# Attention in front of two soft mixtures on one Trainium2 core: the division by the sums, the narrowing of 64-bit weights and the order of all queues are changed

## The chip, the cores and the metric

One core of one Trainium2 chip. The core has TensorE (matrix products, written to PSUM), VectorE (DVE in the profile), ScalarE (ACT), GpSimd (POOL), the queue SP that issues most transfers, and 16 DMA engines. The metric is the device time of one execution in microseconds; the kernel before has a median of 676.77 us in three runs (672.96 to 681.78).

## The reference

```python
# q, k, v: (8, 8, 576, 64) float32
scores = scale * np.matmul(q, k.transpose(0, 1, 3, 2))          # scale = 1/8
scores = np.where(block_i >= block_j, scores, -1e9)             # causal in blocks of 64
scores = scores - np.max(scores, axis=-1, keepdims=True)
attn = np.exp(scores)
attn = attn / (np.sum(attn, axis=-1, keepdims=True) + 1e-09)
out = np.matmul(attn, v)                                        # -> x: (4608, 512)
# soft mixture: logits = x @ phi; softmax over tokens d, over slots c
# slot_input = d.T @ x; 8 experts (relu(slot_input @ w1[e]) @ w2[e]); x = c @ slot_out
# second block: a = x @ w1; b = x @ w2; result = ((a * b) @ w3) @ w_out
```

The weights of the second block come as 64-bit floats.

## The kernel before

The 64 heads are 32 pairs of two heads; the two heads of a pair lie in the upper and lower 64 partitions. Four pairs make a batch (one of the 8 examples). For each pair n the attention does, by the names of the planner:

- `ld`, `ldv`: load q and k (`raw`, 576 KB) and v (320 KB) on SP; `cast` (ScalarE) makes the high part, `sub` (POOL) the low part, so that products run in a fast format with a correction
- `M0` to `M3` (TensorE): rough scores of the high parts, for the maxima; `R0` to `R3` (VectorE) reduce them; `l2` masks the maxima of blocks and reduces again; `mT`, `mc`, `mx` transpose them, copy them out of PSUM and write them as a row (by DMA) into the operand that subtracts them
- `Q0` to `Q3` (TensorE): the scores in three products and that correction; `E0` to `E3` (ScalarE): exponentials into PTa, PTb, PTc
- `P0` to `P4` (POOL): partial sums of the exponentials; `SU` (TensorE) sums over partitions; `sb` (VectorE) adds the result to `Sb`
- `V1`, `V0` (TensorE): products with v; `c1`, `c0` (ScalarE) copy them to `xT`

For each batch b but the last: `sumT` transposes `Sb`, `r` takes reciprocals, `rT` and `rc` transpose them back and copy, `rw` writes them to HBM and `rd` reads them spread over partitions; `sx0` to `sx3` (VectorE) scale the four tiles of `xT`; then `lg` (logits), `lgT`, `L4`, the softmax over slots (`cm` to `cTd`), the softmax over tokens (`LT` to `dnc`), `xn`, `xc` (x in its natural layout) and `S`, `SSu` (slot inputs).

Beside all this, 16 narrowing jobs `b1` to `b4`, `bm` turn 64-bit weights of 128 x 512 into float32 by shifts and masks on VectorE, each loaded by `bl` (512 KB). `win` loads expert weights (2,048 KB) into tiles that the attention no longer needs; the first is loaded at the start. The constants of the start are 374 KB.

PSUM has two double tiles `sc` for Q, one double tile `mx` for M (and `LT`), and two single tiles `pv` for all the rest.

The order on each engine is not found by a scheduler: class `Plan` lists all these operations with engine, duration, what they wait for and a due time (`n * PERIOD + OFF[name]`), and `order()` runs them through a list scheduler; among operations that can start within `LOOK` of the first, the one with the smallest due time (plus `WAIT` for lateness) comes next. `run()` issues in that order, and each engine executes its own queue in order.

After the attention: the last batch's softmaxes (`push_tail`), eight experts with their weights loaded window by window, products of the second block's weights, and a last stage of products of 512 columns (L1210).

The functions that the change touches, with the lines of the profile:

Of the kernel before, what the change touches and what calls it, by code (L numbers as in the profile page):

```python
# [51 lines left out]
OFF = dict(ld=-59.98, ldv=-11.1, cast=-11.65, sub=-2.81, M0=-23.01, M1=-25.68, M2=-15.87, M3=-20.31, l2=61.69,  # L52
           mT=-12.75, Q0=16.46, Q1=14.73, Q2=17.44, Q3=10.38, P0=-30.76, P3=19.54, V1=14.16, V0=59.16, SU=15.87,
           sumT=-32.63, sx=11.53, lg=-1.05, lgT=24.25, cm=55.23, cT=15.16, LT=46.32, dn=40.78, xn=21.48, xstep=5.41,
           S=-15.63, b=30.37)
PERIOD, SWITCH, WAIT = 11.25, 2.51, 22.29
LOOK = dict(PE=0.13, DVE=0.94, ACT=0.32, POOL=2.58, SP=3.66)
BG0, BGS = 10.14, 1.42
MX = ((.26, 1.22), (.21, 1.1), (.15, .83), (.23, .83))
QK = ((1.26, 1.03), (1.03, 1.03), (.59, .71), (.48, .6))  # L60
SLOTS = {"sc": 2, "mx": 1, "pv": 2}


class Plan:
# [3 lines left out]
    def __init__(self, nb):  # L68
# [3 lines left out]
        quarter = lambda x: [f"{x}{i}" for i in range(4)]  # L72
        for n in range(N):
            self.due = lambda t: n * PERIOD + off[t]
            op = lambda name, *a, **k: self.op((name, n), *a, **k)
            at = lambda *names: [(x, n) for x in names]
            op("ld", "SP", .45, old(n - RAW, "sub"), lat=5.5 if n else 2.6)
            op("ldv", "SP", .45, old(n - VB, "V1", "V0"), lat=6)
            op("cast", "ACT", 1.16 if n else .7, at("ld") + old(n - NS, *quarter("Q")))
            op("sub", "POOL", 2.65, at("cast"))  # L80
            for i, (d, r) in enumerate(MX):
                op(f"M{i}", "PE", d, at("cast"), "mx", mode="rows")
                op(f"R{i}", "DVE", r, at(f"M{i}") + old(n - 2, "l2"), free=f"M{i}", due=f"M{i}")
            op("l2", "DVE", .55, at(*quarter("R")) + old(n - 2, "mT"))
            op("mT", "PE", .11, at("l2"), "pv")
            op("mc", "ACT", .25, at("mT") + old(n - 2, "mx"), free="mT", due="mT")
            op("mx", "SP", 1.9, at("mc") + old(n - 2, *quarter("Q")), lat=2.2, due="mT")
# [12 lines left out]
            op("V1", "PE", 2.05, at("E0", "E1", "E2", "ldv"), "pv", mode="cols")  # L100
            op("c1", "ACT", .43, at("V1") + x, free="V1", due="V1")
            op("V0", "PE", .68, at("E0", "E3", "ldv"), "pv", mode="cols")
            op("c0", "ACT", .38, at("V0") + x, free="V0", due="V0")
            op("SU", "PE", .69, at(*(f"P{j}" for j in range(5))), "pv", mode="quarters")
            op("sb", "DVE", .49, at("SU") + (old(n - 1, "sb") if n % NP_B else old(b - 1, "sumT")), free="SU", due="SU")
        for b in range(nb - 1):
# [21 lines left out]
            op("cT", "PE", .28, at("cmul"), "pv")  # L128
            op("cTc", "ACT", .46, at("cT") + old(b - 1, "cTd"), free="cT", due="cT")
            op("cTd", "SP", 1.2, at("cTc"), lat=3, due="cT")  # L130
            op("LT", "PE", .57, at("L4"), "mx")
            op("LTm", "DVE", 1.2, at("LT"), due="LT")
            op("LTe", "ACT", 2.0, at("LTm") + old(b - 1, "dn", "SSu", "Ls"), free="LT", due="LT", late=.1)
            op("Ls", "DVE", .16, at("LTe"), due="LT", late=.2)
            op("dn", "PE", .35, at("LTe"), "pv", mode="few rows")
            op("dnc", "ACT", .29, at("dn") + old(b - 1, "S"), free="dn", due="dn")
            for c in range(5):
                op(f"xn{c}", "PE", .45 if c < 4 else .3, at(*quarter("sx")), "pv", due="xn", late=c * off["xstep"])
                op(f"xc{c}", "ACT", .59, at(f"xn{c}", "lg"), free=f"xn{c}", due="xn", late=c * off["xstep"])
            op("S", "PE", 1.06, at("dnc", *(f"xc{c}" for c in range(5))), "pv", mode="quarters")  # L140
            op("SSu", "DVE", .75, at("S", "LTe"), free="S", due="S")
        for j in range(16):
# [3 lines left out]
            op("bl", "SP", .45, old(j - 1, "b3", "bm"), lat=4, due="b", late=-.5 * PERIOD)  # L146
            op("b1", "DVE", .6, at("bl") + old(j - 1, "b4"), due="b")
            op("b2", "DVE", .85, at("b1"), due="b", late=.1)
            op("b3", "DVE", .85, at("b2"), due="b", late=.2)
            op("bm", "ACT", .67, at("bl") + old(j - 1, "b4"), due="b")  # L150
            op("b4", "DVE", .85, at("b3", "bm"), due="b", late=.3)
        self.due = lambda t: t * PERIOD
# [1173 lines left out]
```

## Time and profile before

| | |
|---|---|
| median of three runs | 676.77 us |
| the profiled execution | 680.79 us, its span 679.0 us |
| TensorE busy | 607.6 us (89%) |
| VectorE busy | 482.9 us (71%) |
| ScalarE busy | 329.1 us (48%) |
| POOL busy | 365.5 us (54%) |
| moved by DMA | 117.00 MB, mean 172 GB/s |

Busy times are unions, so overlapping products count once. The chain that ended last puts 29% of the span on TensorE. The attention takes about the first 405 us. Rows of a timeline give the start, the duration of the group, the engine, the line and the operation, and in brackets how long the engine sat idle before it and who released it.

### The profile page before, as it was taken

What the parts mean: (1) busy time and instruction counts of PE and PEld (TensorE: products, weight loads), DVE (VectorE), ACT (ScalarE), POOL (GpSimd) and SP (SyncE); (2) the same over time, 40 slices, a digit from 0 to 9 for tenths busy, and PEclk for the clock granted to TensorE, in tenths of its full rate; (3) what the DMA queues carried; (4) which work ended last, traced back from release to release, by engine and by line L of the source; (5) the groups of instructions that cost most, each with busy time, mean ns of one, the idle gap of its engine ahead of it and who ended that gap; (6) DMA issues with size and microseconds to landing.
All of it is one profiled execution on the core that took longest, in us unless ns stands there. A gap on an engine that the chain in (4) does not pass through costs nothing. (4 is left out here: it accounts for less than half of the span.)

```text
span 679.0 us, 13657 instructions
## 1 busy us (share of the span) xinstructions
PE 607.6 (89%) x5414; PEld 437.1 (64%) x5414; DVE 482.9 (71%) x692; ACT 329.1 (48%) x628; POOL 365.5 (54%) x280
## 2 busy tenths in 40 slices
PE   3699879989889889889979998769999998999997
PEld 1577666766666666667757765425664676888886
DVE  5688787898898898885675535799933798555550
ACT  2356436646456456446645563345423335445451
POOL 4499686787587587587666650144424322332220
PEclk9999879989889899889989998988999998999999
DMA  8434722643543453442611729999884404555742
GB/s 304 172 106 136 197 87 60 161 138 109 132 150 98 135 157 96 128 133 72 169 57 45 207 94 410 419 367 429 318 307 171 127 1 125 188 192 193 260 147 93
DMA packets 40674, 117.00 MB, mean 172 GB/s; under 512 B 6639, under 2 KB 17031, under 8 KB 38547
## 3 DMA queue, kind: packets, MB, share of 16 engines
q1 hardware_dynamic: 40431, 116.06, 50.3%
q8 instruction: 42, 0.69, 0.4%
q14 instruction: 21, 0.17, 0.1%
q10 hardware_dynamic: 180, 0.07, 0.0%
HBM read 105.80 MB, written 10.47 MB: 171 GB/s over the span
## 5 line engine op out<-in xcount | busy, mean ns | idle before, releaser
L324 DVE TENSOR_REDUCE bm<-mx 128x10 f32<-128x640 f32 (+2 forms) x128 | 126.1, 985 | 61.2 <-PE mx L320 60.0
L359 PE MATMUL sc<-set 64*128 64x320 f32 (+4 forms) x1152 | 121.3, 321 | 0.0
L359 PEld LDWEIGHTS sc<-set 64*128 64x128 f32 x1152 | 96.2, 200 | 10.6 <-issue 7.2
L309 POOL TENSOR_TENSOR set<-raw,set 128x1152 fp32r<-128x1152 f32 x32 | 92.7, 2897 | 11.5 <-ACT set L302 9.7
L1210 PE MATMUL ops<-H,Ph 128*128 128x512 f32 x288 | 91.6, 399 | 3.3 <-ACT H L1114 2.4
L320 PE MATMUL mx<-set 64*128 64x320 f32 (+4 forms) x384 | 59.1, 359 | 23.3 <-DVE bm L324 22.2
L378 POOL TENSOR_TENSOR acc<-PTa,PTb 128x640 f32<-128x640 f32 x32 | 53.6, 1674 | 44.6 <-ACT PTb L367 39.1
L1185 POOL TENSOR_TENSOR Pl<-rot,Ph 128x384 fp32r<-128x384 f32 x24 | 30.3, 1281 | 77.4 <-ACT Ph L1183 77.4
L1210 PEld LDWEIGHTS ops<-H,Ph 128*128 128x128 f32 x288 | 55.0, 191 | 17.3 <-ACT H L1114 2.9
L359 PE MATMUL sc<-shift 64*128 64x320 f32 (+4 forms) x384 | 61.1, 313 | 0.0
L378 POOL TENSOR_TENSOR acc<-acc,PTc 128x640 f32<-128x640 f32 x31 | 53.8, 1736 | 12.0 <-ACT PTc L367 10.1
L320 PEld LDWEIGHTS mx<-set 64*128 64x128 f32 x384 | 33.8, 198 | 38.0 <-DVE bm L324 24.5
L1210 PE MATMUL ops<-H,Pl 128*128 128x512 f32 x144 | 57.6, 400 | 0.0
L367 ACT ACTIVATE PTc<-sc 128x512 f32<-128x512 f32 x64 | 41.3, 645 | 33.1 <-PE sc L359 33.1
L906 PE MATMUL wps<-wo,w 128*128 128x512 f32 x192 | 51.3, 411 | 3.1 <-POOL wo L852 1.7
L458 DVE TENSOR_TENSOR xT<-xT,shift 128x576 f32<-128x576 f32 x28 | 48.7, 1796 | 3.4 <-DMA shift<-rr 3.4
L1213 ACT COPY o<-ops 128x512 f32<-128x512 f32 x36 | 21.1, 587 | 58.5 <-PE ops L1212 58.2
L906 PEld LDWEIGHTS wps<-wo,w 128*128 128x128 f32 x192 | 35.3, 192 | 20.7 <-issue 5.8
L367 ACT ACTIVATE PTb<-sc 128x1024 f32<-128x1024 f32 x32 | 32.8, 1024 | 27.2 <-PE sc L359 27.2
L393 PE MATMUL pv<-PTc,v 128*64 128x256 f32 (+1 forms) x256 | 44.9, 429 | 0.3 <-DVE Sb L421 0.3
L378 POOL TENSOR_TENSOR acc<-PTa,PTc 128x256 f32<-128x256 f32 x31 | 28.1, 906 | 27.5 <-ACT PTc L367 27.4
L367 ACT ACTIVATE PTa<-sc 128x1024 f32<-128x1024 f32 x32 | 32.8, 1026 | 16.4 <-PE sc L359 16.3
(247 smaller groups left out, 1217.3 us busy)
## 6 DMA issues: line engine op xcount, KB each, us to landing
win<-in_moe_w SPq DMA_DIRECT2D x16, 2048.0 KB
raw<-in_qk SPq DMA_DIRECT2D x32, 576.0 KB
v<-in_v SPq DMA_DIRECT2D x32, 320.0 KB
rot<-cs SPq DMA_DIRECT2D x48, 192.0 KB
out<-o SPq DMA_DIRECT2D x11, 768.0 KB
raw<-in_moe_w SPq DMA_DIRECT2D x16, 512.0 KB
w3raw<-in_w3T SPq DMA_DIRECT2D x16, 512.0 KB
shift<-rr SPq DMA_DIRECT2D x14, 576.0 KB
```

Source lines behind the costliest of these rows:

```text
L309: self.nc.gpsimd.tensor_tensor(lo, self.raw.pop(n), hi.bitcast(F32), op=ALU.subtract)
L320: self.nc.tensor.matmul(self.mx_b[:, h, o:o + kn], lhsT=qh[r, q0:q0 + 128], rhs=kh[r, k0:k0 + kn], start=True, stop=True)
L324: self.nc.vector.tensor_reduce(self.bmb[n % 2][:, :, o:o + m // 64], self.mx_b[:, :, 0:m].rearrange("p h (n k) -> p h n k", k=64), axis=AX ...
L359: self.nc.tensor.matmul(ps[:, h, o0:o0 + w], lhsT=lt[r, k] if i < 3 else lt[r], rhs=rt[r, q0:q0 + w], start=i == 0, stop=i == 3)
L367: self.nc.scalar.activation(out=out, in_=ps[:, :, 0:sum(g[3] for g in self.UNITS[u])], func=AF.Exp, scale=SCALE)
L378: eng.tensor_tensor(acc[:, :, lo:hi], a, b, op=ALU.add)
L393: mm(ps[64 * h:64 * h + 64, q0 - lo:q1 - lo], lhsT=v[:, 128 * j + 64 * h:128 * j + 64 * h + 64], rhs=pt[:, h, o:o + q1 - q0], start=j == 0 ...
L458: self.nc.vector.tensor_tensor(x, x, self.rb[:, p], op=ALU.mult)
L906: nc.tensor.matmul(p, lhsT=a[:, o], rhs=b, start=c + i == 0, stop=c == 7 and i == 2)
L1185: eng.tensor_tensor(Pl[:, k], p, Ph[:, k].bitcast(F32), op=ALU.subtract)
L1210: nc.tensor.matmul(ps, lhsT=a[:, k, r], rhs=b[:, k], start=n == 0, stop=False)
L1213: nc.scalar.copy(o[:, t], ps)
```

## The change

1. **Division.** `sumT`, `rT`, `rw`, `rd` go. `r` is one reciprocal of the whole `Sb` (128 x 320) into a `pv` tile; `rc` and `rl` combine it into the operand `rA`, `rb0` to `rb4` spread it over partitions by a product with a selection matrix `rsel`, into `pv` tiles, and `sx0` to `sx4` multiply `xT` by them from there. EPS is added in the batch's last `sb`.
2. **Narrowing.** The working tile `u` of `b1` to `b4` is a `pv` tile in place of one in SBUF.
3. **Masking.** The masked maxima are overwritten by two constant writes in place of an addition of `lmask`.
4. **PSUM.** `mx` is gone; three double tiles `sc` serve M, Q and LT.
5. **Start.** The constants are loaded by a planned operation `kl`, and `kc`, `kd`, `ke` build what is made of them.
6. **Plan.** Due times depend on the pair's place in its batch, TensorE takes its operations strictly by due time, `LOOK` and `WAIT` are new for each engine; waits for buffers have moved from the copies to the products in front of them.

```diff
-OFF = dict(ld=-59.98, ldv=-11.1, cast=-11.65, sub=-2.81, M0=-23.01, ...
+OFF = dict(ld=(-216.25, -345.22, 6.22, 92.03), ldv=(29.88, 253.15, 394.31, -307.64), cast=(46.44, 145.88, 221.53,
...
-SLOTS = {"sc": 2, "mx": 1, "pv": 2}
+SLOTS = {"sc": 3, "pv": 2}
...
+            if n == 0:
+                op("kl", "SP", 2.9, [("ld", 1)], lat=2.3, due="ld")
+                op("kc", "ACT", 2.2, at("cast", "kl"), due="cast", late=.1)
...
-                op(f"M{i}", "PE", d, at("cast"), "mx", mode="rows")
+                op(f"M{i}", "PE", d, at("cast") + old(n - 2, "l2"), "sc", mode="rows")
...
-            op("sumT", "PE", .33, [("sb", last)], "pv")
-            op("r", "DVE", .78, at("sumT") + old(b - 1, "rT"), free="sumT", due="sumT")
-            op("rT", "PE", .11, at("r"), "pv", due="sumT", late=.1)
...
-                op(f"sx{p}", "DVE", .8, at("rd") + [("c1", NP_B * b + p), ("c0", NP_B * b + p)], due="sx", late=.1 * p)
+            op("r", "DVE", 2.8, [("sb", last)] + old(b - 1, *(f"rb{i}" for i in range(5))), "pv")
+            op("rc", "ACT", .46, at("r"), due="r", late=.1)
+            op("rl", "DVE", .5, at("rc"), free="r", due="r", late=.2)
...
+                op(f"rb{i}", "PE", .3 if i < 4 else .43, at("rl") + x + [("kd", 0), ("ke", 0)], "pv")
+                op(f"sx{i}", "DVE", .65 if i < 4 else .4, at(f"rb{i}"), free=f"rb{i}", due=f"rb{i}")
...
-            op("b1", "DVE", .6, at("bl") + old(j - 1, "b4"), due="b")
+            op("b1", "DVE", .6, at("bm"), "pv", due="b")
...
     def op_l2(self, n, _):
-        t = self.st_p.tile([128, 2, 45], F32, tag="l2", name="l2")
-        self.nc.vector.tensor_tensor(t, self.bmb[n % 2], self.lmask, op=ALU.add)
+        t = self.bmb[n % 2]
+        for i in (8, 24):
+            self.nc.vector.memset(t[0:64, :, i:i + (6 if i == 8 else 12):5 if i == 8 else 11], -1e30)
...
+    def op_r(self, b, slot):
+        ps = self.st["r"] = self.pv_b[slot][:, 0:320]
+        self.nc.vector.reciprocal(ps, self.Sb[:, 0:320])
...
+    def op_rl(self, b, _):
+        self.nc.vector.scalar_tensor_tensor(self.rA, self.st["r"], self.low[:, 0:1], self.rT.bitcast(F32), op0=ALU.mult, op1=ALU.add)
+
+    def op_rb(self, b, slot, i):
+        ps = self.st["rb", i] = self.pv_b[slot]
+        for p, g, o, c, w in ((i, 0, 0, 0, 320), (i, 1, 320, 64, 192)) if i < 4 else [(p, 1, 64 * p, 256, 64) for p in range(4)]:
+            self.nc.tensor.matmul(ps[:, o:o + w], lhsT=self.rsel[:, g, p], rhs=self.rA[:, c:c + w], start=True, stop=True)
+
+    def op_sx(self, b, _, i):
+        ps = self.st["rb", i]
+        if i < 4:
+            x, r = self.xTb[b % 2][:, i, 0:512], ps
+        else:
+            x, r = self.xTb[b % 2][:, :, 512:S], ps[:, 0:256].rearrange("p (g t) -> p g t", g=4)
+        self.nc.vector.tensor_tensor(x, x, r, op=ALU.mult)
...
-            u = self.u64 = self.cv.tile([128, 512], I32, tag="u", name="u64")
+            u = self.u64 = self.attn.pv_b[slot].bitcast(I32)
```

What now stands where. VectorE, around the scaling of a batch in the middle, first in the kernel before (u is the narrowing's tile in SBUF, `shift` holds the factors read back from HBM):

```order
L324 TENSOR_REDUCE bm_119<-mx 128x2x7
L837 SCALAR_TENSOR_TENSOR wB<-m_2765,u_2735 128x512
L324 TENSOR_REDUCE bm_119<-mx 128x2x8
L458 TENSOR_TENSOR xT_130<-xT_130,shift 128x576 x4
L324 TENSOR_REDUCE bm_119<-mx 128x2x5
L421 TENSOR_TENSOR Sb<-Sb,pv_116 128x320
L828 TENSOR_SCALAR u_2971<-raw_2828 128x512
L830 SCALAR_TENSOR_TENSOR u_2971<-raw_2828,u_2971 128x512
L324 TENSOR_REDUCE bm_119<-mx 128x2x5
```

The same engine at the scaling in the changed kernel (pv_114 and pv_115 are the two small PSUM tiles, `shift` is rA):

```order
L852 SCALAR_TENSOR_TENSOR wB<-m_3178,pv_114 128x512
L453 SCALAR_TENSOR_TENSOR Sb<-pv_115,Sb 128x320
L460 RECIPROCAL pv_114<-Sb 128x320
L466 SCALAR_TENSOR_TENSOR shift<-pv_114,low,shift 128x320
L479 TENSOR_TENSOR xT_127<-xT_127,pv_114 128x512
L479 TENSOR_TENSOR xT_127<-xT_127,pv_115 128x512
L479 TENSOR_TENSOR xT_127<-xT_127,pv_114 128x4x64
L352 TENSOR_REDUCE bm_117<-sc_113 128x2x7
L479 TENSOR_TENSOR xT_127<-xT_127,pv_115 128x512
L479 TENSOR_TENSOR xT_127<-xT_127,pv_114 128x512
L352 TENSOR_REDUCE bm_117<-sc_111 128x2x5
L352 TENSOR_REDUCE bm_117<-sc_113 128x2x8
```

The narrowing's last step and the batch's addition now stand in front of one reciprocal, the scalings read PSUM, and one reduction stands between them.

TensorE, from Q0 of the next pair but one to the spread (L471) in the changed kernel; the sums of the batch's last pair (L437), a maxima transpose (L363) and Q2 (L388) stand directly ahead (sc are the three double tiles):

```order
L388 MATMUL sc_113<-set_65 128x448 x6
L388 MATMUL sc_113<-shift 128x448 x2
L388 MATMUL sc_113<-set_65 128x64 x6
L388 MATMUL sc_113<-shift 128x64 x2
L422 MATMUL pv_115<-PTc,v 64x320 x2
L422 MATMUL pv_115<-PTa,v 64x320 x2
L422 MATMUL pv_115<-PTb,v 64x320 x2
L422 MATMUL pv_115<-PTb,v 64x192 x2
L426 MATMUL pv_115<-PTa,v 64x64 x2
L388 MATMUL sc_112<-set_65 128x256 x6
L388 MATMUL sc_112<-shift 128x256 x2
L471 MATMUL pv_114<-shift 128x320
```

In the kernel before, the transposed sums stood there directly behind the slot inputs (L573), with the other transpose (L441) behind the next Q3, Q1 and Q2:

```order
L571 MATMUL pv_117<-xT_130,d 32x512 x4
L573 MATMUL pv_117<-xT_130,d 32x128 x4
L429 MATMUL pv_116<-ident,Sb 128x128 x3
L320 MATMUL mx<-set_68 128x320 x2
L359 MATMUL sc_114<-set_67 128x256 x6
L359 MATMUL sc_114<-shift 128x256 x2
L359 MATMUL sc_113<-set_67 128x320 x6
L359 MATMUL sc_113<-shift 128x320 x2
L359 MATMUL sc_113<-set_67 128x192 x6
L359 MATMUL sc_113<-shift 128x192 x2
L441 MATMUL pv_117<-ident,r 40x128
```

So four transposes have left TensorE's queue, and between the sums and the first product that needs the reciprocals stand a maxima transpose, the groups Q2 and Q0, a V1 and a Q3.

SP at the start, in the changed kernel (the constants are xT to sel):

```order
L316 DMA raw<-in_qk 128x1152 x2
L320 DMA v<-in_v 128x640 x2
L862 DMA win_160<-in_moe_w 128x4096
L320 DMA v<-in_v 128x640
L291 DMA xT_128<-in_rt_const 6x1216 x2
L292 DMA ident<-in_ident 128x128
L293 DMA phib<-in_phib 128x256
L294 DMA phi<-in_phi 128x128
L295 DMA sel_67<-in_sel 128x32
L316 DMA raw<-in_qk 128x1152 x2
L837 DMA raw_206<-in_moe_w 128x1024
```

and before:

```order
L289 DMA raw<-in_qk 128x1152
L266 DMA lmask<-in_lmask 128x90
L267 DMA ident<-in_ident 128x128
L265 DMA xT_130<-in_rt_const 6x1216 x2
L268 DMA phib<-in_phib 128x256
L269 DMA phi<-in_phi 128x128
L270 DMA sel_69<-in_sel 128x32
L289 DMA raw<-in_qk 128x1152
L293 DMA v<-in_v 128x640 x3
L822 DMA raw_174<-in_moe_w 128x1024
L847 DMA win_176<-in_moe_w 128x4096
L289 DMA raw<-in_qk 128x1152 x2
```

The constants stood behind the first `raw` and now stand behind two `raw`, three `v` and the first window.

## Rows read from the trace of the kernel before

**Rows 1.** Stretches: length, busy us of PE, PEld, DVE, ACT, POOL; PEclk, DMA share, GB/s.

```profile
257.40:309.00 51.60, 45.92 (x528) 34.38 (x524) 42.99 (x54) 28.11 (x53) 36.99 (x27) 0.93 0.40 118
...
356.80:405.10 48.30, 48.30 (x598) 35.97 (x593) 24.61 (x44) 29.60 (x61) 31.51 (x29) 1.00 0.35 102
sum 379.76, PE 348.20 PEld 259.09 DVE 294.46 ACT 212.41 POOL 276.40; mean PE 43.52 PEld 32.39 DVE 36.81 ACT 26.55 POOL 34.55
```

**Rows 2.** Waits of PE, 54.9 to 357 us: total us, times, longest.

```profile
PE pv L467 <- DVE xT L458: 15.4, 8, 2.3
PE mx L320 <- DVE bm L324: 8.3, 9, 3.0
PE pv L429 <- DVE Sb L421: 5.8, 3, 1.9
```

**Rows 3.** Timeline of DVE at the scaling of a batch.

```profile
292.57 7.07 DVE L458 TENSOR_TENSOR xT<-xT,shift 128x576 f32<-128x576 f32 x4
```

**Rows 4.** DVE lines over the span: durations ns min/median/max, first and last start.

```profile
L458 DVE TENSOR_TENSOR xT<-xT,shift x28: 746/1702/3184, 88.5 to 389.8; 128x576 f32<-128x576 f32 x28
L830 DVE SCALAR_TENSOR_TENSOR u<-raw,u x16: 681/1369/2997, 14.2 to 281.8; 128x512 int32<-128x512 int32 x16
L828 DVE TENSOR_SCALAR u<-raw x16: 419/818/1773, 13.1 to 280.7; 128x512 int32<-128x512 int32 x16
L421 DVE TENSOR_TENSOR Sb<-Sb,pv x24: 470/472/489, 49.4 to 407.5; 128x320 f32<-128x320 f32 x24
L437 DVE RECIPROCAL r<-r x7: 403/403/405, 68.9 to 372.0; 128x40 f32<-128x40 f32 x7
L499 DVE RECIPROCAL csm<-csm x7: 190/191/191, 106.2 to 404.3; 128x5 f32<-128x5 f32 x7
```

**Rows 5.** Timeline of PE: after a wait, and the same groups without one.

```profile
275.34 0.85 PE L359 MATMUL sc<-set 64*128 64x256 f32 x6
...
278.53 0.73 PE L359 MATMUL sc<-set 64*128 64x320 f32 x6
...
323.03 0.55 PE L429 MATMUL pv<-ident,Sb 128*128 128x128 f32 x3
...
323.76 0.51 PE L359 MATMUL sc<-set 64*128 64x256 f32 x6
...
325.56 0.71 PE L359 MATMUL sc<-set 64*128 64x320 f32 x6
```

**Rows 6.** Timeline of PE: Q0, M0, V1, M3, Q3, SU by their first rows.

```profile
280.56 0.88 PE L359 MATMUL sc<-set 64*128 64x448 f32 x6
...
281.85 0.50 PE L320 MATMUL mx<-set 64*128 64x192 f32 x4
282.28 0.76 PE L393 MATMUL pv<-PTc,v 128*64 128x320 f32 x4
...
284.48 0.42 PE L320 MATMUL mx<-set 64*128 64x256 f32 x4
284.74 0.60 PE L359 MATMUL sc<-set 64*128 64x256 f32 x6
...
285.39 0.30 PE L408 MATMUL pv<-PTc,ones 128*32 128x128 f32 x2
```

**Rows 7.** A stretch of the last stage, products of 512 columns.

```profile
590.00:640.00 50.00, 50.00 (x215) 40.30 (x215) 26.58 (x43) 23.41 (x49) 12.95 (x10) 1.00 0.62 210
```

**Rows 8.** Timelines of ACT and PE at the start: third cast, first maxima, first score product.

```profile
19.55 1.15 ACT L302 CAST set<-raw 128x1152 fp32r<-128x1152 f32 x1 [5.77 <-DMA raw<-in_qk]
20.61 0.25 ACT L339 CAST mT<-pv 10x128 fp32r<-10x128 f32 x1
...
25.34 1.35 PE L359 MATMUL sc<-set 64*128 64x448 f32 x6
```

**Rows 9.** A stretch of the expert stage.

```profile
460.00:480.00 20.00, 20.00 (x115) 13.57 (x112) 18.38 (x28) 8.85 (x16) 8.41 (x7) 0.93 0.99 407
```

**Rows 10.** The page's group of the exponentials of Q0.

```profile
L367 ACT ACTIVATE PTa<-sc 128x1024 f32<-128x1024 f32 x32 | 32.8, 1026 | 16.4 <-PE sc L359 16.3
```

More of the change, by code (lines that the diff above doesn't have):

```diff
@@ L99, in __init__ @@
             x = old(b - 2, "S", *(f"xn{c}" for c in range(5)))
[L100 to L105, printed above, removed]
+            op("V1", "PE", 2.05, at("E0", "E1", "E2", "ldv") + x, "pv", mode="cols")
+            op("c1", "ACT", .43, at("V1"), free="V1", due="V1")
+            op("V0", "PE", .68, at("E0", "E3", "ldv") + x, "pv", mode="cols")
+            op("c0", "ACT", .38, at("V0"), free="V0", due="V0")
+            op("SU", "PE", .69, at(*(f"P{j}" for j in range(5))) + ([] if n % NP_B else old(b - 1, "r")), "pv", mode="quarters")
+            op("sb", "DVE", .49, at("SU"), free="SU", due="SU")
         for b in range(nb - 1):
@@ L164, in order @@
         ops, INF = self.ops, 1e18
-        free = dict(PE=1., DVE=2., ACT=2., POOL=3., SP=.7)
+        free = dict(PE=4., DVE=2., ACT=2., POOL=3.5, SP=.7)
         slots, held, done, mode, out = {r: [0.] * n for r, n in SLOTS.items()}, {}, {}, None, []
         waits, then, ready = {k: len(o["after"]) for k, o in ops.items()}, {}, {e: {} for e in free}
+        row = deque(sorted((k for k in ops if ops[k]["eng"] == "PE"), key=lambda k: (ops[k]["due"], k)))
         for k, o in ops.items():
@@ L212, with __init__ @@
 class Attn:
-    def __init__(self, tc, ctx, io, nb, keep, after_scores=None, background=()):
-        self.after_scores, self.background = after_scores, background
+    def __init__(self, tc, ctx, io, nb, keep, rest, windows=True):
+        self.rest, self.windows = rest, windows
+        rest.attn = self
         self.tc, self.nc, self.io, self.nb = tc, tc.nc, io, nb
@@ L285, in constants2, with op_kl, op_kc, op_kd @@
             nc.gpsimd.memset(t[64:128, :, S:SP], 0.0)
+    def op_kl(self, n, _):
+        nc, io = self.nc, self.io
+        for h in range(2):
+            nc.sync.dma_start(out=self.stage[64 * h:64 * h + 6, 0:640 + S], in_=io["rt_const"])
+        nc.sync.dma_start(out=self.ident, in_=io["ident"])
+        nc.sync.dma_start(out=self.phib, in_=io["phib"])
+        nc.sync.dma_start(out=self.phi, in_=io["phi"])
+        nc.sync.dma_start(out=self.keep["sel32"], in_=io["sel32"])
+    def op_kc(self, n, _):
+        self.nc.scalar.copy(self.CT.rearrange("p a b -> p (a b)"), self.stage[:, 0:640])
+        for t in self.Xb:
+            self.nc.scalar.copy(t, self.xconst)
+    def op_kd(self, n, _):
+        v = self.ident.rearrange("p (g h x) -> p g h x", g=2, h=2)
+        for g in range(2):
+            a, b = (v[:, g, :, x:x + 4].unsqueeze(3).to_broadcast([128, 2, 4, 64]) for x in (0, 4))
+            self.nc.gpsimd.tensor_tensor(self.rsel[:, g].rearrange("p x (h d) -> p h x d", h=2), a, b, op=ALU.add)
+    def op_ke(self, n, _):
+        nc = self.nc
+        v = self.ident.rearrange("p (j x) -> p j x", x=32)
+        nc.vector.tensor_reduce(self.low[:, 0:1], v[:, :, 4:8], axis=AX.XY, op=ALU.add)
+        nc.vector.tensor_scalar(self.low[:, 1:2], self.low[:, 0:1], -2.0, 1.0, op0=ALU.mult, op1=ALU.add)
     def op_ld(self, n, _):
@@ L813, in narrow, with background @@
         return dst
-    def background(self, j, step):
+    def background(self, j, step, slot):
         nc = self.nc
@@ L1227, in setup @@
     keep["cs"] = dp.tile([48, nb * S], F32, name="cs")
-    keep["rr"] = [dp.tile([8, 640], F32, name=f"rr{i}") for i in range(2)]
     sp = ctx.enter_context(tc.tile_pool(name="sets", bufs=1, side="right"))
@@ L1248, in attn_only @@
         with ExitStack() as c2:
-            Attn(tc, c2, io, nb, keep, None, rest.background).run()
+            Attn(tc, c2, io, nb, keep, rest, False).run()
         rest.cv_ctx.close()
@@ L1259, in full @@
         with ExitStack() as c2:
-            Attn(tc, c2, io, nb, keep, rest.load_expert, rest.background).run()
+            Attn(tc, c2, io, nb, keep, rest).run()
         rest.run(out)
```

198 lines of the change are left out of this document (80 added, 118 removed).

## The prediction

> **What bounds the kernel now.** I read the page first: TensorE is busy 89% of the span and leads the chain, and a second stage behind the attention lives on transfers. The change lies in the attention, which ends at about 405 us, so I cut that part into its eight batches of four pairs [rows 1]. From the first score product at 25.34 us to 405.10 TensorE works 348.20 of 379.76 us, so it stands idle 31.6 us. The last batch has no idle time at all (48.30 of 48.30), one with narrowing on VectorE has 5.7 (51.60 less 45.92). So TensorE is the bound wherever it is fed, and what there is to gain is its waits. The view of waits [rows 2] says who causes them between 54.9 and 357 us: products of logits wait for the scaling of xT (15.4 us), maxima for the reduction that frees their only PSUM tile (8.3 us), and the transposed sums for VectorE's addition (5.8 us). These 29.5 us are nearly all of the 31.6, and VectorE ends every one.
>
> Why is VectorE late when it is busy only 71%? The timeline shows four scalings back to back that take 7.07 us [rows 3]; meanwhile no reduction runs and no maxima tile comes free. The same instruction took 0.75 us at best, 1.70 in the median and 3.18 at worst, and a step of the narrowing 0.68, 1.37 and 3.00. The addition into Sb, which has one input in PSUM and one in SBUF, took 0.470 to 0.489 us in all 24 cases [rows 4]. So instructions with two SBUF inputs are stretched by something that leaves those with a PSUM input alone; POOL works through the same stretch on SBUF tiles.
>
> A wait costs more than itself. After the last of the three waits for the sums (1.9 us) three score groups took from 275.34 to 278.53, 3.19 us; the same groups took 1.80 us (323.76 to 325.56) where nothing had waited: 1.39 us lost [rows 5]. [...]
>
> **The change part by part, in TensorE's time.**
>
> *Scaling and reciprocals.* The four scalings from SBUF (28 in all, 48 us by the median) become 28 of 512 columns and seven of 256 with the factor in PSUM. From the addition of 320 columns at 0.47 I scale to 0.7 and 0.4: 22 us. Against that VectorE now takes reciprocals of 320 columns. The reciprocal of 40 columns took 0.403 and that of 5 took 0.191, 6.06 ns a column, so 2.1 us; the other bound is 320/40 of 0.403, 3.2 us. With the combination after it (320 columns, 0.47) VectorE comes out some 8 us lower in total at 2.1 and about level at 3.2, but what counts is that no block of 7 us stands in its queue. The 15.4 us and the 5.8 us go; the write to HBM and the read back go too, and SP loses three issues a batch. TensorE pays: eight products of 320 or 192 columns and four of 64 in place of four transposes. A product of 512 columns takes 50.00/215 = 0.23 us in the last stage [rows 7]; two of half that width I take at 0.3, and the four small ones at 0.4, 1.6 together; the transposes that go took 0.55 for three [rows 5], so about 0.75 for four: +0.8 a batch, **+5.6 us** in seven (bounds 3 and 9).
>
> *Narrowing in PSUM.* Three of its four steps lose their second SBUF input and should take the 0.68 of their best case: 16 x (4 x 0.7) = 45 us against 16 x (0.82 + 3 x 1.37) = 79 by the medians, the last two steps taken like the second. No TensorE work depends on it, so its own gain is nothing; what it frees is the queue in front of reductions and sums. It now holds one of the two small PSUM tiles for about 2.8 us, twice a batch.
>
> [...] The first step, one input and a constant, had a best case of 0.419 in SBUF [rows 4], less than the 0.68 of the others. [...]
>
> *One pool of PSUM tiles.* Maxima may now take any of three double tiles. The 8.3 us of waits go with them. The price could be a score product that waits for a tile held by a reduction; in the new order a tile is asked for again only three groups later, and with no 7 us block ahead a reduction is done by then. I take none; the bound is the old 8.3.
>
> *Masking* by two constant writes in place of a sum, and the new constants built once: VectorE and POOL have room (42.99 and 36.99 of 51.60 in the fullest kind of batch), so nothing; above, 32 times the 0.47 of a whole addition, 15 us of VectorE, still off the path.
>
> *The clock.* The eleven waits of the first and third row of [rows 2] fall in nine places of over 1.3 us; at 1.2 us each, 11 us come back.
>
> *The start.* SP now issues the 2 MB window ahead of the constants. In the old order the third raw pair, behind 5.0 MB, had landed at 19.55 [rows 8]. The new constants end after 4.49 MB, where 5.62 were then through: 19.55 x 0.80 = 15.6 us. They are copied in three pieces (say 2 us), and the first maxima are written by DMA, which took from 20.61 to 25.34 at most, 4.7 us. So the first score product comes at about 22.5 instead of 25.34: **-2.5 us** (bounds -4 and +2).
>
> *New waits.* The tightest new chain is sums, addition, reciprocal, copy, combination, spread: 0.47 + 2.1 + 0.47 + 0.47 and five hand-overs that I put at 0.1, 4.0 us (5.1 with the dear reciprocal). In TensorE's new order Q2, Q0, V1 and Q3 stand between. Their start-to-start times are 1.29 for Q0, 2.20 for V1, 0.65 for Q3 [rows 6], and Q2, wider than Q3, at least that: 4.8 us. It fits, with 0.8 to spare or 0.3 too little. Other chains (maxima, DMA write, scores) have a whole pair's work between. No plan is kept to the tenth of a microsecond, so I charge 1 us a batch: **+7** (bounds 0 and 29, next part).
>
> Sum against the profiled execution (span 679.0, 680.8 with what lies around it): -15.4 - 5.8 - 8.3 - 11 = -40.5; +5.6 - 2.5 + 7 = +10.1; together -30.4, so 650.4. That execution lies 4.0 above the median of 676.77; against the median: 646.4, forecast **647 us**. The stage behind moves up with it: its transfers run at 407 GB/s with a share of 0.99 at 460 to 480 us [rows 9], but they start when the last scores release the windows, and that moment moves.
>
> **The rivals.**
>
> 1. *The new chain takes the place of the old wait.* ScalarE's copy of the reciprocals stands in its queue behind the exponential of Q0, 1.03 us [rows 10], which starts only when Q0 is done. If that and the dear reciprocal meet, the spread starts about 1.4 late, and with the clock's 1.2 it costs 2.6 a batch, 18 us; if the small tiles add as much again per narrowing, 29. Against -37.4 without new waits that leaves -19 to -8: 658 to 669. For it: the chain fits by tenths. Against: the order puts five microseconds of other products there.
>
> 2. *Slower: the narrowing stays stretched and now holds a PSUM tile.* If what stretches it isn't the second SBUF input but the strided int32 read (both stand in the same rows), the four steps keep 0.82 + 3 x 1.37 = 4.9 us, 2.1 over plan, and for that time TensorE has one small tile for V, SU, transposes and spread. With the clock that is up to 3.3 us, 16 times 53: 676.8 - 37.4 + 53 = 692. It decides (slower than before) from 2.3 us a narrowing. Against: the best case 0.68 has the same strides; the scalings have none and are stretched the same.
>
> 3. *Hidden.* The attention ends early but the later stage doesn't move. It would take loads that are already late by themselves; 0.99 in [rows 9] speaks for it, their release by the last scores against. 670 to 677.
>
> 4. *All waits go.* The same without the +7 and with the start's best bound: 638.
>
> **How the numbers follow.** Forecast and rival 4 are one case, 638 to 660, 0.68. Rival 1 0.18, rival 2 0.07, rival 3 0.07. The range takes the first case and half of rival 1: 638 to 664. About 2% is what a measurement of this kernel can tell from no change, that is 663. Faster: 0.68 and half of rival 1, 0.77. Same: the rest of rival 1 and most of rival 3, 0.15. Slower: 0.08.
>
> **What would show it.** Scalings of 512 columns at 0.7 us without spread and reciprocals at 2.1 to 3.2; narrowing steps near 0.7 with no long ones; a batch of about 46 us between logits (45.92 of work, less 2 of slow clock, plus 0.8 and 1) instead of 51.6; waits of TensorE for the scaling gone and its clock near 1.00 throughout; the first score product before 24 us. Wrong it would be by a PSUM-bound step of VectorE that is still stretched, by waits of the spread for the combination over 1.5 us, or by waits for a small tile during the narrowing.

## The result and the profile after

The changed kernel takes 627.69 us in the median of four runs (625.52 to 628.81); the kernel before took 679.27 us in four executions (672.96 to 682.31). The ratio is 0.925, with a 95% interval of 0.917 to 0.933. The direction was forecast, the size was not: 51.6 us were saved where the forecast saw 30, and the time lies under the range of 638 to 664.

The page's first part, of the changed kernel (busy us, share of the span, instructions):

```profile
span 627.0 us, 13824 instructions
PE 592.8 (95%) x5470; PEld 432.6 (69%) x5470; DVE 420.7 (67%) x724; ACT 331.3 (53%) x630; POOL 336.7 (54%) x282
```

TensorE was busy 607.6 us of 679.0 before and is now 592.8 of 627.0. VectorE has shed 62 us and POOL 29, although POOL's program is the same but for two additions at the start.

The attention as one stretch, from the first score product to the end of the last, first of the kernel before, then of the changed one (columns as in [rows 1]):

```profile
25.34:402.60 377.26, 345.70 (x3965) 257.82 (x3962) 292.63 (x389) 210.97 (x391) 273.90 (x199) 0.95 0.41 121
```

```profile
19.87:351.60 331.73, 331.55 (x4014) 253.64 (x4018) 236.10 (x418) 214.39 (x394) 246.22 (x200) 1.00 0.35 112
```

Idle time of TensorE fell from 31.6 to 0.2 us, its work from 345.70 to 331.55, and the column of its granted clock shows 1.00. (The profile's record of the clock starts only at 29.23 us in this execution, and the column counts what lies ahead of it as 1.00, as it does for 0 to 20 us; the last experiment comes back to that.) One batch from logits to logits, to be held against the 51.60 us of [rows 1]:

```profile
158.12:201.12 43.00, 43.00 (x532) 32.75 (x530) 32.00 (x58) 28.35 (x53) 32.47 (x26) 1.00 0.36 114
```

Lines of VectorE in the changed kernel (ns min/median/max, first and last start), answering to [rows 4]:

```profile
L479 DVE TENSOR_TENSOR xT<-xT,pv x35: 420/680/690, 67.4 to 328.7; 128x512 f32<-128x512 f32 x28, 128x256 f32<-128x256 f32 x7
L843 DVE TENSOR_SCALAR pv<-raw x16: 675/684/695, 24.9 to 335.8; 128x512 int32<-128x512 int32 x16
L845 DVE SCALAR_TENSOR_TENSOR pv<-raw,pv x16: 695/695/697, 25.6 to 336.5; 128x512 int32<-128x512 int32 x16
L460 DVE RECIPROCAL pv<-Sb x7: 2160/2161/2161, 62.5 to 320.3; 128x320 f32<-128x320 f32 x7
```

The spread is gone: what ran from 0.75 to 3.18 us now takes 0.68 to 0.69 each time (0.42 for the pieces of 256 columns). Among the waits of TensorE (total us, times, longest), none of the three rows of [rows 2] has a successor inside the attention; the largest of the whole span lie at the start and behind it:

```profile
PE so L1028 <- ACT win L1019: 4.4, 5, 2.4
PE sc L348 <- ACT set L329: 2.8, 2, 2.6
PE sc L348 <- ACT set L332: 2.6, 1, 2.6
PE pv L363 <- DMA ident<-in_ident: 1.6, 1, 1.6
```

What went on beside the instructions with two SBUF inputs stands in the trace of before, in the timeline of VectorE and POOL at one scaling:

```profile
192.13 1.24 POOL L378 TENSOR_TENSOR acc<-PTa,PTc 128x256 f32<-128x256 f32 x1
192.71 4.38 DVE L458 TENSOR_TENSOR xT<-xT,shift 128x576 f32<-128x576 f32 x2
193.34 3.14 POOL L309 TENSOR_TENSOR set<-raw,set 128x1152 fp32r<-128x1152 f32 x1
196.44 2.06 POOL L378 TENSOR_TENSOR acc<-PTa,PTb 128x640 f32<-128x640 f32 x1
```

The second scaling ends at 197.09, 0.61 us behind the end of POOL's instruction of 193.34 (196.48); POOL's next takes 2.06 us, where the same one takes 1.56 in the changed kernel. The whole trace of before has the same pattern: 22 of the 28 scalings began when an instruction of POOL had 0.3 us or more still to run, and every one of them ended 0.61 to 0.62 us behind the end of that instruction; the other six took 0.75 us. In the changed kernel 32 of the 35 scalings run beside POOL and take no longer than the rest (0.68 to 0.69 us beside it and 0.68 without it for 512 columns, 0.42 both ways for 256). So in the kernel before both lost: the scalings took up to 3.18 us in place of 0.75, POOL's addition 2.06 in place of 1.56. What holds them up beside each other is not shown.

### The profile page after: what moved, and what is told of

The parts are those of the page before. It is cut to its first block, busy times and chain, and to the rows that moved or that the text cites. A ratio compares the mean times of both kernels' runs of the same rounds, so it can differ in the third digit from the quotient of the medians.

```text
span 627.0 us, 13824 instructions
## 1 busy us (share of the span) xinstructions
PE 592.8 (95%) x5470; PEld 432.6 (69%) x5470; DVE 420.7 (67%) x724; ACT 331.3 (53%) x630; POOL 336.7 (54%) x282
## 4 chain that ended last, share of the span: by engine, by line
PE 86%; DVE 9%; DMA 2%; ACT 1%; issue 1%; SPq 0%; DVEq 0%; ACTq 0%
PE sc L388 19%; PE ops L1225 16%; PE pv L422 14%; PE wps L921 7%; PE sc L348 6%; PE pv L437 3%; PE pv L547 3%; PE pv L471 2%; PE so L1028 2%; PE pv L488 2%; DMA win<-in_moe_w 2%; PE h L1001 1%; PE ops L1227 1%; PE pv L363 1%; DVE f L827 1%; PE pv L594 1%
## 5 line engine op out<-in xcount | busy, mean ns | idle before, releaser
L352 DVE TENSOR_REDUCE bm<-sc 128x10 f32<-128x640 f32 (+2 forms) x128 | 123.5, 988 | 47.7 <-PE sc L348 33.8
L388 PE MATMUL sc<-set 64*128 64x320 f32 (+4 forms) x1152 | 118.1, 312 | 0.1
L388 PEld LDWEIGHTS sc<-set 64*128 64x128 f32 x1152 | 92.3, 190 | 9.5 <-issue 3.2
L336 POOL TENSOR_TENSOR set<-raw,set 128x1152 fp32r<-128x1152 f32 x32 | 84.9, 2654 | 8.9 <-ACT set L329 5.9
L407 POOL TENSOR_TENSOR acc<-PTa,PTb 128x640 f32<-128x640 f32 x32 | 49.9, 1559 | 59.3 <-PE pv L437 56.4
L388 PE MATMUL sc<-shift 64*128 64x320 f32 (+4 forms) x384 | 60.8, 306 | 0.0
L348 PE MATMUL sc<-set 64*128 64x320 f32 (+4 forms) x384 | 53.0, 348 | 6.7 <-ACT set L329 2.8
L407 POOL TENSOR_TENSOR acc<-acc,PTc 128x640 f32<-128x640 f32 x31 | 48.4, 1562 | 1.3
L396 ACT ACTIVATE PTa<-sc 128x1024 f32<-128x1024 f32 x32 | 32.8, 1025 | 30.7 <-PE sc L388 15.6
L396 ACT ACTIVATE PTc<-sc 128x640 f32<-128x640 f32 (+1 forms) x64 | 40.7, 651 | 12.2 <-PE sc L388 12.0
L422 PE MATMUL pv<-PTc,v 128*64 128x320 f32 (+1 forms) x256 | 44.4, 425 | 0.0
L348 PEld LDWEIGHTS sc<-set 64*128 64x128 f32 x384 | 32.1, 197 | 17.8 <-issue 7.7
L431 ACT COPY xT<-pv 128x320 f32<-128x320 f32 (+1 forms) x64 | 25.5, 398 | 35.0 <-PE pv L426 28.9
L388 PEld LDWEIGHTS sc<-shift 64*128 64x128 f32 x384 | 38.6, 191 | 1.0 <-DMA shift<-mT 0.4
```

What stands on the lines that cost most here:

```text
L336: self.nc.gpsimd.tensor_tensor(lo, self.raw.pop(n), hi.bitcast(F32), op=ALU.subtract)
L348: self.nc.tensor.matmul(ps[:, h, o:o + kn], lhsT=qh[r, q0:q0 + 128], rhs=kh[r, k0:k0 + kn], start=True, stop=True)
L352: self.nc.vector.tensor_reduce(self.bmb[n % 2][:, :, o:o + m // 64], self.st.pop(("M", n, i))[:, :, 0:m].rearrange("p h (n k) -> p h n k", ...
L388: self.nc.tensor.matmul(ps[:, h, o0:o0 + w], lhsT=lt[r, k] if i < 3 else lt[r], rhs=rt[r, q0:q0 + w], start=i == 0, stop=i == 3)
L396: self.nc.scalar.activation(out=out, in_=ps[:, :, 0:sum(g[3] for g in self.UNITS[u])], func=AF.Exp, scale=SCALE)
L407: eng.tensor_tensor(acc[:, :, lo:hi], a, b, op=ALU.add)
```

## The experiments

Two theories stood against each other. **Theory 1**: the operands carry the gain, because a VectorE instruction with one input in PSUM takes no longer beside POOL (0.68 to 0.69 us in the scalings of the changed kernel) and POOL no longer beside it. **Theory 2**: the new order of the queues carries it.

### 1. Operands back in SBUF, order kept

The narrowing alone:

```diff
-            u = self.u64 = self.attn.pv_b[slot].bitcast(I32)
+            u = self.u64 = self.cv.tile([128, 512], I32, tag="u", name="u64")
```

> The changed kernel with the narrowing's working tile u back in SBUF; the plan and the order of every queue stay as they are. Theory 1 (the operands carry the gain: a VectorE instruction with two SBUF inputs and a POOL instruction hold each other up, and a PSUM input takes VectorE out of that): the second to fourth step go from 0.69 back to about 1.4 us, POOL's `sub` from 2.65 back towards 2.9, VectorE gains some 30 us of busy time, reductions come late and TensorE waits again for maxima tiles: 633 to 642 us. Theory 2 (the new order carries the gain, since it puts enough other products in front of whatever VectorE must deliver): VectorE grows the same but TensorE does not wait: 626 to 630 us.

Measured: 634.15 us (632.79 to 636.38), 6.5 more than the changed kernel. Groups of VectorE in this kernel (busy us, mean ns), and behind them its waits of TensorE:

```profile
L843 DVE TENSOR_SCALAR u<-raw 128x512 int32<-128x512 int32 x16 | 21.3, 1333 | 0.0
L845 DVE SCALAR_TENSOR_TENSOR u<-raw,u 128x512 int32<-128x512 int32 x16 | 16.0, 1002 | 0.6
```

```profile
PE pv L363 <- DVE m L360: 2.5, 7, 0.5
PE pv L471 <- DVE shift L466: 2.1, 6, 0.4
```

All four steps are stretched again (1.33, 1.00, 0.98 and 1.37 to 1.38 us in the mean, 0.68 to 0.70 in the changed kernel), POOL goes from 336.7 to 349.7 us, VectorE from 420.7 to 451.8; but the waits are short, 0.5 us at most. So 31 us of VectorE cost 6.5 of time.

The scalings alone, read from a copy that ScalarE makes:

```diff
+        w, ps = 512 if i < 4 else 256, self.Lg[:, i % 2, 0:512]
+        self.nc.scalar.copy(ps[:, 0:w], self.st["rb", i][:, 0:w])
```

> The changed kernel, but ScalarE copies each spread tile out of PSUM into SBUF (five copies a batch) and the scaling reads the copy. Theory 1: the scalings of 512 columns go from 0.68 to about 1.5 us, the block in front of the logits grows by 3 to 4 us a batch, TensorE waits for it and runs at the lower clock for a while after: 2 to 3 us a batch, 642 to 650 us. Theory 2: the order has a whole V1, V0 or score group between spread and logits; the copies add 0.5 us each to the chain and little of it is seen: 628 to 634 us.

Measured: 659.30 us (658.27 to 661.04). That is 9 us above the range of theory 1, a first sign that the copies cost something of their own. Both edits at once:

> Both of the former at once: plan, order and PSUM pool of the changed kernel, operands in SBUF as before. Theory 1: the two losses add up, 648 to 662 us, that is, well over half of the gain of some 50 us is gone. Theory 2: 628 to 637 us, the order alone keeps most of the gain.

Measured: 666.06 us (665.13 to 667.51), 4 above the range of theory 1; ratio to before 0.979 (0.974 to 0.983). The losses add up, 38 of the 51.6 us, and theory 2 falls as the main cause; 13 to 14 us of the gain stay without the operands, for the new order, the PSUM pool and the start together. But the waits of the kernel with copies (659.30 us) warn that its cause is mixed:

```profile
PE pv L471 <- ACT Lg L475: 18.9, 13, 2.9
```

TensorE waits for ScalarE's copies. So the scalings were given their second SBUF input without a copy, by a tile of ones (`w`) and one column of the spread tile:

```diff
-        self.nc.vector.tensor_tensor(x, x, r, op=ALU.mult)
+        self.nc.vector.scalar_tensor_tensor(x, w, ps[:, 0:1], x, op0=ALU.mult, op1=ALU.mult)
```

> The changed kernel, where a scaling multiplies xT by an SBUF tile of ones and by the first column of the spread tile in PSUM: two whole inputs from SBUF, no copy by ScalarE, still released by the spread product. It leaves out that each token gets its own factor. The run before it with copies lost 31 us, but TensorE there waited 18.9 us for ScalarE's copies, not for the scalings. If the operands alone are worth much: scalings at 1.2 us and more as there, waits of the spread products for their PSUM tile, 636 to 648 us. If the copies were the loss: 627 to 633 us.

Measured: 653.76 us (652.03 to 658.01), 26.1 more, 6 above the range expected. The operand is the cause, the copies were worth the other 5. The changed instruction is not: the 14 of its 28 scalings of 512 columns that no instruction of POOL overlapped took 0.74 to 0.75 us (two of them in a row, at 215.65, 1.41). Its waits, the attention as one stretch, and the timeline of one such wait:

```profile
PE pv L472 <- DVE xT L481: 14.1, 7, 2.3
```

```profile
20.10:380.30 360.20, 345.76 (x4012) 262.69 (x4016) 256.06 (x418) 213.55 (x392) 251.76 (x200) 0.96 0.32 103
```

```profile
210.06 4.67 DVE L481 SCALAR_TENSOR_TENSOR xT<-Lg,pv,xT 128x512 f32<-128x512 f32 x3 [1.21 <-PE pv L472]
...
211.38 3.07 POOL L337 TENSOR_TENSOR set<-raw,set 128x1152 fp32r<-128x1152 f32 x1
...
214.78 0.80 PE L472 MATMUL pv<-shift 128*128 128x320 f32 x2 [2.26 <-DVE xT L481]
215.51 1.17 PE L389 MATMUL sc<-set 64*128 64x320 f32 x6
```

Three scalings, two of 512 columns and one of 256, take 4.67 us beside POOL, TensorE waits 2.26 us, and the score group behind it takes 1.17 us, where six such products take 0.70 elsewhere in this batch (at 210.21). The stretch grew by 28.5 us over the changed kernel's: 14.3 of idle time and 14.2 of work, at a granted clock of 0.96. The 14.1 us of waits are six of 2.3 us, one in each of six batches, and one of 0.5; with all 14.2 us of work put down to the clock, some 2.4 come on top of each wait of 2.3, an estimate.

### 2. One tile for the maxima, order kept

```diff
-SLOTS = {"sc": 3, "pv": 2}
+SLOTS = {"sc": 2, "mx": 1, "pv": 2}
```

(and `M` and `LT` take the slot `mx`)

> The changed kernel with the maxima (and LT) confined to one double PSUM tile and the scores to the other two, as before; order by due times unchanged. If the free choice of tiles is what removed the 8.3 us of waits for the maxima tile: the waits for reductions come back, 8 us and as much again of slow clock, 636 to 645 us. If it was VectorE's shorter queue: reductions are prompt, but two groups of maxima in a row must wait for one reduction of 0.7 to 1.2 us; where the new order sets M groups side by side that shows, elsewhere not: 628 to 634 us.

Measured: 708.83 us, ratio 1.041 (1.035 to 1.046): slower than the kernel before, far outside both expectations. Waits of TensorE (read in its longest execution, with a span of 717.4):

```profile
PE sc L348 <- DVE bm L352: 38.3, 46, 1.3
PE sc L348 <- ACT dT L571: 7.6, 6, 1.3
```

VectorE is no busier than before (423.8 us) and prompt; 46 waits of 0.8 us come from the order itself, which sets groups of maxima closer than one tile allows. So the pool of three tiles is no small part with a price of 8.3 us: this order, as planned, cannot be had without it.

### 3. VectorE's work taken out of the kernel before

The 28 scalings left out:

```diff
-        self.nc.vector.tensor_tensor(x, x, self.rb[:, p], op=ALU.mult)
+        pass
```

> The kernel before without the 28 scalings of xT (the division by the sums is left out; reciprocals, their transposes, write and read back stay). Theory 1 (VectorE's long blocks cause the waits in the old order): the 15.4 us of waits of the logits go, about half of the waits for maxima and sums too, and 1.2 to 2 us of slow clock with each: 645 to 655 us. Theory 2 (the old order itself leaves no room between what is made and who needs it): other waits come in their place, 660 to 672 us.

Measured: 655.08 us (649.30 to 656.06). In place of the narrowing's steps, one constant write:

```diff
-        if step == 1:
+        if step in (1, 2, 3):
+            return
+        elif step == 4:
+            nc.vector.memset(w[:, dc, f:f + 512], 0.01)
```

> The kernel before with one constant write in place of the four narrowing steps (the values of the second block's weights are left out; loads and the ScalarE step stay). Theory 1: some 75 us of VectorE go, the waits for maxima (8.3) and sums (5.8) go, those for the scalings get shorter: 652 to 664 us. Theory 2: 668 to 680 us.

Measured: 660.08 us (659.22 to 668.16). Both:

> The kernel before with both left out. Theory 1: TensorE has no wait left in the attention, a batch takes the 42 to 43 us of pure work, 632 to 642 us: what is left against 627.7 is the start (5.5) and a few changes of product kind. Theory 2: the old order with one maxima tile keeps waits of its own, 645 to 660 us.

Measured: 637.25 us (635.67 to 641.27), all three as theory 1 had it, the first at the upper edge of its range. That is 25 and 20 us alone, 43 together. The attention of the last kernel as one stretch:

```profile
23.40:358.20 334.80, 329.73 (x3964) 246.86 (x3962) 183.69 (x316) 210.93 (x390) 246.64 (x200) 0.99 0.46 136
```

The old order, with its one maxima tile, needs 334.8 us when VectorE is prompt; the new kernel needs 331.7 with VectorE's work in it. The old order was not bad, it had no answer to a VectorE that was late. Not run was the old order with the operands in PSUM: these kernels take the work out and do not make it prompt. The new masking and the lost trip of the reciprocals through HBM were not taken apart either.

### 4. The slack of the new chain

```diff
-        self.nc.vector.scalar_tensor_tensor(self.rA, ...)
+        for _ in range(2):
+            self.nc.vector.scalar_tensor_tensor(self.rA, ...)
```

> The changed kernel with the combination `rl` executed twice (the second writes the same values): 0.55 us more between the sums and the spread. In the changed kernel's trace the combination ends 0.67 us before the first spread product, in all steady batches alike. If the chain has that slack, nothing moves: 627 to 629.5 us. If the profile's gap is taken up by hand-overs, TensorE waits up to 0.55 in each of seven batches and loses clock with it: 632 to 642 us.

Measured: 626.49 us (625.69 to 627.77), 0.5 us under the range expected: nothing moves. The gap can be read in the changed kernel's timeline:

```profile
193.71 0.52 ACT L463 ACTIVATE shift<-pv,low 128x320 fp32r<-128x320 f32 x1
194.27 0.55 DVE L466 SCALAR_TENSOR_TENSOR shift<-pv,low,shift 128x320 fp32r<-128x320 f32 x1 [0.86 <-ACT shift L463]
194.82 0.62 PE L388 MATMUL sc<-set 64*128 64x256 f32 x6
195.28 0.28 PE L388 MATMUL sc<-shift 64*128 64x256 f32 x2
195.49 0.76 PE L471 MATMUL pv<-shift 128*128 128x320 f32 x4
```

The combination ends at 194.82, the spread starts behind Q3 at 195.49. With the reciprocal executed twice instead:

```diff
-        self.nc.vector.reciprocal(ps, self.Sb[:, 0:320])
+        for _ in range(2):
+            self.nc.vector.reciprocal(ps, self.Sb[:, 0:320])
```

> The changed kernel with the reciprocal executed twice: 2.16 us more on the same chain. With a slack of 0.67 TensorE waits 1.5 us in each of seven batches, 10.5 us; and by the run with scalings from two SBUF inputs (14.1 us of waits cost 26.1 us, that is 1.7 us of slow clock for each wait of 2.0) it costs 7 times 1.5 to 1.7 more: 646 to 650 us. If a wait costs only itself: 637 to 639 us. If the chain has more room than the gap shows: under 634 us.

Measured: 636.86 us (634.54 to 639.14), 9.2 more. That is the case in which a wait costs only itself. Its waits and its attention:

```profile
PE pv L472 <- DVE shift L467: 8.6, 7, 1.2
```

```profile
20.10:359.00 338.90, 330.16 (x4012) 252.18 (x4016) 251.21 (x425) 214.05 (x393) 245.95 (x200) 1.00 0.34 110
```

Seven waits of 1.2 us, and the granted clock stays at 1.00; work is 330.16 against 331.55. The wait is 1.2 and not 1.5 because ScalarE's copy, for which the combination waited 0.86 us, holds it up for 0.59 here:

```profile
198.42 0.55 DVE L467 SCALAR_TENSOR_TENSOR shift<-pv,low,shift 128x320 fp32r<-128x320 f32 x1 [0.59 <-ACT shift L464]
```

So the slack is 2.16 - 1.23 = 0.93.

### 5. The start

```diff
-        for i, (t, after) in enumerate(((20, []), ...
+        for i, (t, after) in enumerate(((20, [("sub", 4)]), ...
```

> The changed kernel with the first expert window (2 MB) issued on SP after the low part of pair 4 instead of between the first v tiles; it is not needed before 357 us. In the changed kernel the first maxima transpose waits 1.62 us for ident and the rough scores of pair 2 wait 2.64 us for their cast, both behind that window. If the start is set by bytes on the DMA queue (2 MB at about 410 GB/s are 4.9 us), the first score product comes near 16 us instead of 19.87 and the whole ends 3 to 4 us earlier, 623.5 to 625 us. If it is set by the chain of reductions, copies and the DMA write of the maxima, it comes at 19 or later: 626.5 to 628 us.

Measured: 621.54 us (620.35 to 622.90), 2 under the range expected, ratio to before 0.920 (0.915 to 0.924); the kernel with the doubled combination, run beside it, took 626.49, and no run of the one reaches those of the other. Moving the window out of the way is worth 5 to 6 us, and this version beats both kernels. Its timeline at the start, after that of the changed kernel:

```profile
14.68 0.37 PE L363 MATMUL pv<-ident,m 128*10 128x128 f32 x1 [1.62 <-DMA ident<-in_ident]
...
17.70 0.85 PE L348 MATMUL sc<-set 64*128 64x192 f32 x4 [2.64 <-ACT set L329]
...
19.87 1.49 PE L388 MATMUL sc<-set 64*128 64x448 f32 x6
```

```profile
12.90 0.38 PE L363 MATMUL pv<-ident,m 128*10 128x128 f32 x1
...
14.67 0.85 PE L348 MATMUL sc<-set 64*128 64x192 f32 x4 [1.40 <-ACT set L329]
...
16.89 1.49 PE L388 MATMUL sc<-set 64*128 64x448 f32 x6
```

The first score product comes 3.0 us earlier, so the window's bytes on the queue held the start up by that much, not by the 4 expected. The other 2 to 3 us lie behind it (the stretch from the last score product to the end took 271.6 us in this execution, 275.4 in the changed kernel's, 274.0 in that with the doubled combination); whether the window has a part in that stays open.

### 6. Changes of kind on TensorE

```diff
+            if not a and not b and c and d and row[i + 1][0] in ("V0", "V1", "SU", "xn0", "xn1", "xn2", "xn3", "xn4"):
+                row[i + 1], row[i + 2] = row[i + 2], row[i + 1]
```

(a to d: whether the four groups from place i on are score products)

> The changed kernel with TensorE's row of work altered in one respect: where two groups that are not score products stand side by side and two groups of score products follow, the second of the pair goes behind the first score group. The same work, each moved by one group; by the planner's kinds 327 changes of kind instead of 268 (the kernel before had 296). In the kernel before without scalings and narrowing TensorE worked 329.7 us in the attention; with 7.4 us more for the spread the changed kernel should have had 337, and it had 331.6, so 5.6 us went for 28 changes fewer, 0.2 us each. If that is the cause, 59 more cost 6 to 12 us of busy time of TensorE: 633 to 640 us. If the price of a change is nothing and the 5.6 us were slow clock left in that run, 626 to 630 us. Waits in the trace have to be taken off.

Measured: 667.20 us (665.34 to 667.95), but most of it is another thing: four narrowing jobs ended only behind the last score product, and two products of the last batch waited for them.

```profile
PE pv L647 <- DVE wB L857: 26.7, 2, 21.5
```

Within the attention there is no wait:

```profile
19.87:361.70 341.83, 341.03 (x4012) 256.14 (x4016) 225.25 (x402) 213.18 (x389) 245.96 (x200) 0.99 0.33 104
```

341.83 against 331.73: 10.1 us, of which 9.5 are TensorE's work (341.03 against 331.55). The 0.99 looks like slow clock that would have to come off. Cut in two, the stretch has it at its start:

```profile
19.87:28.50 8.63, 8.63 (x59) 7.91 (x59) 5.50 (x10) 4.74 (x7) 5.58 (x4) 0.50 0.45 150
28.50:361.70 333.20, 332.40 (x3955) 248.23 (x3959) 219.76 (x392) 208.44 (x382) 240.38 (x197) 1.00 0.33 103
```

But the changed kernel was as slow there, and only its record of the clock says nothing ahead of 29.23 us. Its first six score products took 1.49 us, the row of 19.87 in section 5, and the same group took 0.87 later on; in this run the six took 1.49 as well. First this run, then the changed kernel:

```profile
19.87 1.49 PE L393 MATMUL sc<-set 64*128 64x448 f32 x6
```

```profile
346.56 0.87 PE L388 MATMUL sc<-set 64*128 64x448 f32 x6
```

So the slow clock of the start is in both and drops out: 9.5 us for 59 changes, 0.16 a change. That the changes alone make it up, and not what else the moved groups stand beside, is not shown.

## Why the forecast was right in its mechanism and wrong in its sum

Against the profiled executions (680.79 and 628.81 us, 52.0 apart):

| term | forecast | found |
|---|---|---|
| waits in the attention | -29.5 | -31.4 |
| slow clock after them | -11 | -15.5 to -17.7 |
| spread products | +5.6 | +8.5 |
| the rest of TensorE's work (fewer changes of kind) | none | -4.9 to -7.1 |
| start | -2.5 | -5.5 |
| new waits | +7 | 0 |
| behind the attention | 0 | -1.0 |

**Right.** The reading of [rows 4], that a second SBUF input is what stretches and a PSUM input is what cures, holds in both directions (26 and 6.5 us back when undone; 25 and 20 gained in the old order, though by taking the work out). Scalings, narrowing and reciprocals took what was estimated (0.68, 0.69, 2.16). The waits went, all of them. Rival 2, a narrowing that stays stretched and holds a tile, did not happen. Rival 3 did not either: the later stage moved up whole (276.4 us from the last score product to the end before, 275.4 now). Rival 4, that all waits go, was what happened, and even its 638 lay 10 above the result.

**Right, but too narrow.** The reason given, a second SBUF input, does not cover the first step of the narrowing. It has one tile as input and was stretched all the same, from 0.419 to 1.773 us [rows 4]; with its result in PSUM it takes 0.68 each time.

**The first step's best case.** The first step of the narrowing takes 0.684 us with its result in PSUM, against 0.419 at best from SBUF. But from SBUF in the same order its mean was 1.333, so the best case was of little use in this kernel.

**Step 1 that failed: new waits.** I charged 1 us a batch, since 0.8 us of slack looked too thin to be kept. It was read well (0.67 in the trace, 0.93 by the doubled reciprocal), and it is kept: the gap between combination and spread is 0.67 to 0.68 us in all seven batches. Five of the six stretches from logits to logits take 43.0 us and the first takes 42.6, where the forecast had 46. The charge of 7 us had no row behind it, and 0 was found: 7 us of the miss.

**Step 2: the clock.** I took 1.2 us for a place with a wait, from one pair of rows that itself gave 1.39 [rows 5]. No run shows the 1.2: the waits of 2.3 us with the tile of ones come out at some 2.4 each, and those of 1.2 us with the doubled reciprocal left the clock at 1.00. In the attention of the kernel before the granted clock reads 0.50 in nine stretches, which sum up to this (columns as in [rows 1]):

```profile
sum 34.11, PE 31.02 PEld 26.21 DVE 20.92 ACT 7.67 POOL 18.54; mean PE 3.45 PEld 2.91 DVE 2.32 ACT 0.85 POOL 2.06
```

With 0.50 read as half speed, half of the 31.02 us of work is lost: 15.5, or 1.7 a place, an estimate (a group of six score products took 1.49 us at 0.50 and 0.87 at 1.00). That there are nine, as forecast, is in part luck. Eight follow the waits that I counted; the wait of 1.95 us at 246.83 has none, and the ninth follows a wait of 3.0 us for a maxima tile, which I had left out. The other way to it gives 17.7: work fell from 345.70 to 329.73 when VectorE's load was taken out, and the 329.73 still hold slow clock (0.99 in that stretch) that I put at 1.7, one place. 4.5 to 6.7 us of the miss.

**Step 3: the start.** I put the landing of the constants at 15.6 us by bytes; the transpose that needs `ident` ran at 14.68, and the write of the maxima, for which I allowed 4.7, took from 16.22 to 19.87 at most. 3 us.

**Step 4: TensorE's own work.** The spread cost more (all groups of the line together 13.6 us by their start-to-start times, 1.94 a batch, the old transposes 5.1). But the forecast counted no gain from the order on TensorE. Its work fell by 22.6 us beside the spread (345.70 + 8.5 - 331.55); less the clock, 4.9 to 7.1 are left (the expectation of the last experiment had 5.6, with 7.4 for the spread). The changes of kind, 28 fewer (268 in place of 296 by the planner's kinds), are worth 4.5 of them at the 0.16 of the last experiment; what the rest is stays open. The clock and this term can be told apart only within the ranges of the table; their sum, 22.6, is firm.

The range failed for the same reason: its lower end took all waits away but kept the clock at 11 and the start at 4, both too small, and had nothing for TensorE's own work.

## What to carry to other kernels

Where VectorE's instructions scatter by a factor of four (0.75 to 3.18 us in the scalings), look at what POOL does in the same microseconds: in this kernel the narrowing's working tile in PSUM in place of SBUF took 31 us off VectorE's busy time and 13 off POOL's, although the best case of its first step went from 0.419 to 0.68. Take what slow clock costs from the granted clock over the whole stretch, not from one wait, and hold the durations of like products against it, since its record can start late (at 29.23 us in the changed kernel's trace). And an order of the queues, the number of its tiles and the slack of its chains belong together: undoing one of them under an order made for the others can cost more than the whole change gained (81 us for the one maxima tile, against 51.6).

## What the runs showed of the hardware that was not expected

- Seven waits of TensorE of 1.2 us cost themselves and left its granted clock at 1.00; six of 2.3 us left it at 0.96, and the run took 26.1 us more for 14.1 us of waits.
- A scaling with two SBUF inputs that began when an instruction of POOL had 0.3 us or more still to run ended 0.61 to 0.62 us behind the end of POOL's instruction, in all 22 cases of the kernel before; the other six took 0.75 us.
- VectorE and POOL lose together: with the scalings and the narrowing out of the kernel before, POOL's busy time fell from 365.5 to 335.5 us with no change in its own program; in the changed kernel it is 336.7.
- Moving one group of products of another kind between two score groups cost TensorE 0.16 us a change.
